# Sinkhorn-sorted attention and a squared-ReLU FFN: the first batch's q transposes, the filler matmuls and the opening order of the head pairs

## The chip, the cores and the metric

One core of a Trainium2 chip runs the whole program. The metric is device microseconds for one execution, and lower is better. TensorE is called PE below, VectorE DVE, ScalarE ACT, GpSimd POOL and SyncE SP, as in the profile.

## What is computed

For each of 4 batches and 8 heads, an 8x8 matrix is put through five rounds of exponential, row normalization and column normalization (Sinkhorn). It then mixes the eight blocks (96 rows each) of k and of v. Each q block attends to its own mixed block, and the result, put back to 3072 tokens of 512 channels, goes through a feed-forward network (FFN).

```python
for _ in range(5):
    P = P - np.max(P, axis=-1, keepdims=True)
    P = np.exp(P)
    P = P / (np.sum(P, axis=-1, keepdims=True) + 1e-09)
    P = P / (np.sum(P, axis=-2, keepdims=True) + 1e-09)
k_sorted = np.einsum('bhij,bhjcd->bhicd', P, k_b).reshape(B, H, S, D)   # v likewise
scores = scale * np.matmul(q_b, k_sb.transpose(0, 1, 2, 4, 3))
attn = softmax(scores); o = np.matmul(attn, v_sb)                       # B,H,S,D = 4,8,768,64
x = o.transpose(0, 2, 1, 3).reshape(3072, 512)
h = np.maximum(x @ w_in, 0.0)                                           # w_in 512 x 2048
out = h * h @ w_out                                                     # w_out 2048 x 512
```

## The kernel before

The work is cut into pieces, and each piece is handed to a planner (`Plan`, lines 50 to 117) as an `Op` with an engine, a cost in microseconds and the ops it depends on. The planner lays all ops out in time with these costs. For PE it has two queues: attention ops, strictly in the order in which they were added, and FFN ops. It takes the attention op at the head when that one is due (its `due` against the number of FFN chunks so far) and nearly ready, or when the FFN could not go on. The instructions are then issued in the order of the planned begins (line 836), so this order is what the engines run; the waits between them are put in by the framework.

A head pair (two heads) of one batch is a `Unit`. Its stages, with the letters that the string `FIRST` (line 19) uses, are:

- q (`s_q`, L385): twelve PE transposes of q into the PSUM tile `qtp` (L395), then a copy to `qT`.
- K and V (`s_sort`, L423): twelve matmuls of k or v with `w_all`, which holds the Sinkhorn weights spread over blocks (L437, tile `tp`), then a cast to `ksT` or `vsT`.
- S (`s_sc`, L461): eight score matmuls into `scp` (L473), then two exponentials on ACT (L489), one for each head, into `et`.
- T (`s_vt`, L497): transposes of the mixed v (L505, tile `vbp`), then a copy to `vs`.
- A (`s_av`, L570): eight matmuls into `oup` (L584), then a reciprocal and a multiply on DVE (L594, L595), the norm, into `ao`.
- X (`s_xt`, L614): transposes of `ao` into `xtp` (L632), then a copy to `xT`, which the FFN reads.

A capital letter in `FIRST` puts the copy on ACT, a small one on DVE.

The FFN runs over 8 groups of 384 tokens (`ffn_unit`, L650). A group has 16 up chunks of four matmuls (L663, tile `hp`), each followed by a ReLU on ACT (L671) and a square on DVE (L674), and then 12 down chunks (L691).

The opening: the sort matrix arrives, five Sinkhorn rounds alternate between ACT (`exp`, L331) and DVE (L299 to L301), then PE transposes and spreads the result (L343, L349) and DVE multiplies it into `w_all` (L360). In the meantime q, k and v of batch 0 arrive by DMAs that POOL issues in a fixed order (lines 258 to 286): q's first 64 partitions (which are the first half of the sequence's blocks), k and v of head pairs 0 to 3, the first quarter of `w_in`, q's second 64 partitions, the rest of `w_in`, `w_out`, then batch 1. ACT also makes `sel` (L308) from the identity that POOL builds between its first two DMAs. PE transposes the first half of q for the four head pairs during Sinkhorn (line 745). Then `FIRST` runs the stages of the first half of batch 0's tokens, and only when its last X is done can the FFN start. The second half of batch 0 is laid between the FFN chunks of group 0 (`lay(0, (1,), ...)`, line 821), and there each unit starts with the transposes of its second half of q (line 793).

While nothing else is there for PE, it runs filler matmuls on a tile of ones: 20 of 256 columns at the start (`warm`, L319), and, until the first FFN chunk, some before each op ahead of which the planner sees a gap of more than 0.5 us:

```python
if filled and not started and op.gap > 0.5:
    fill(int(op.gap / 0.12), 128)
```

PSUM is shared out in three pools: `ps1` with one buffer (`qtp`, `pT`, `vbp`, `xtp`), `ps2` with two buffers of [128, 2, 512] fp32 (`scp`, `oup`, later `tp`, `vnp`), and `psf` with three buffers of [128, 512] fp32 (`pt_ps`, the early `tp`, the FFN's `hp` and `op`, and the fillers' tile `fill`). The planner mirrors them with the rings `r1`, `r2` and `rf` (lines 33 to 47).

Of the kernel before, what the change touches and what calls it, by code (L numbers as in the profile page):

```python
# [8 lines left out]
FP32 = mybir.dt.float32  # L9
BF16 = mybir.dt.bfloat16  # L10
# [5 lines left out]

FIRST = ("V0 K0 v1 K1 t0 S0 k2 v2 S1 t1 A0 V3 K3 t2 S2 S3 t3 A1 X0 A2 X1 A3 X2 x3")


class Op:
# [98 lines left out]
def kernel(  # L121
# [12 lines left out]
    B, H, S, D = q.shape  # L134
# [3 lines left out]
    NA = S // 128  # L138
    C0 = 128 // NB
# [12 lines left out]
    att = ctx.enter_context(tc.tile_pool(name="att", bufs=2))  # L152
    ffn = ctx.enter_context(tc.tile_pool(name="ffn", bufs=2))
    ps1 = ctx.enter_context(tc.tile_pool(name="ps1", bufs=1, space=bass.MemoryType.PSUM))
    ps2 = ctx.enter_context(tc.tile_pool(name="ps2", bufs=2, space=bass.MemoryType.PSUM))
    psf = ctx.enter_context(tc.tile_pool(name="psf", bufs=3, space=bass.MemoryType.PSUM))


    ctx.enter_context(tc.manual_schedule(engines={
        mybir.EngineType.PE, mybir.EngineType.DVE, mybir.EngineType.Activation,  # L160
        mybir.EngineType.SP}))

    plan = Plan()
    rvn, rvb = Ring(2), Ring(3)
# [28 lines left out]
    nc.sync.dma_start(out=p_sb, in_=sort_net.rearrange("b h i j -> (b h) i j"))  # L193


    ones = const.tile([128, 256], BF16)
    nc.vector.memset(ones, 1.0)  # L197
    ident = const.tile([128, 128], BF16)
    nc.vector.memset(ident, 0.0)
# [58 lines left out]
    first = plan.add("DMA", 4.3, lambda e: None)  # L258
    landed["last"] = first
    load(0, 0, 0, H, slice(0, 64))  # L260
    id_op = plan.add("POOL", 0.4, lambda e: make_identity(nc, ident, nomemset=True))
    mask = const.tile([128, C0], BF16)

# [11 lines left out]
        if g == 0:  # L275
            plan.add("POOL", 1.0, make_mask, [id_op])
    load_w_in(0)
    load(0, 0, 0, H, slice(64, 128))
    for g in range(1, 4):
        load_w_in(g)  # L280
    for g in range(4):
# [31 lines left out]
    def fill(n, w):  # L313
        for _ in range(n):
            nc.tensor.matmul(  # L315
                out=tiles["fill"][:, 0:w], lhsT=ones[:, 0:128], rhs=ones[:, 0:w],
                start=True, stop=True)

    def warm(e):  # L319
        tiles["fill"] = psf.tile([128, 512], FP32, tag="pf", name="fill")  # L320
        fill(20, 256)


    slot, old = rf.take()
    rf.use(slot, plan.add("PE", 4.3, warm, [plan.add("DVE", 1.1, lambda e: None)]))

    exps = []
    step = plan.add("SP", 2.25, lambda e: None)
# [1 line left out]
    for it in range(5):  # L330
        step = plan.add("ACT", 0.26, lambda e: nc.scalar.activation(  # L331
            out=p_sb, in_=p_sb, func=AF.Exp), [step])
        exps.append(step)
        if it == 0:
            plan.add("ACT", 0.9, make_sel, [step, id_op])
        step = plan.add("DVE", 0.72, lambda e: sink_norm(e, 0), [step])
        step = plan.add("DVE", 0.76, lambda e, it=it: sink_norm(e, 1, it == 4), [step])

# [44 lines left out]
    def s_q(b, hp, p0, p1, due=0, after=None, eng=AD):  # L385

        n = p1 - p0
        t = {}

        def mm(e):  # L390
            qb = qkv[b][0]
            t["p"] = ps1.tile([128, NA, n], BF16, tag="p1", name="qtp")
            for a in range(NA):
                for h in range(2):
                    nc.tensor.transpose(  # L395
                        out=t["p"][64 * h:64 * (h + 1), a, :],
                        in_=qb[p0:p1, 2 * hp + h, D * a:D * (a + 1)],
                        identity=ident[p0:p1, p0:p1])
            if p0 == 0:
                tiles["qT", b, hp] = att.tile(  # L400
                    [128, NB, NA, C0], BF16, tag="qT", name="qT", bufs=6)

        def ev(e):
            copy(e, tiles["qT", b, hp][:, p0 // C0:p1 // C0, :, :],
                 t["p"].rearrange("p a (i c) -> p i a c", c=C0))

        if b == 0:
            dep = landed[b, 0, 0, p0]
        else:
            dep = landed[b, 0, HP * (2 * hp // HP), 0]  # L410
        s1, old = r1.take()
        if p0 == 0:
            qTs[b, hp], oldq = rqT.take()
        else:
            oldq = []
        pe = plan.add("PE", 0.04 + 0.0023 * n, mm, [dep, id_op] + old, due, mode="col")
        readers[b].append(pe)
        op = one_of(eng, cost_b(NA * n), ev, [pe, after] + oldq)
        r1.use(s1, pe, op)
        rqT.use(qTs[b, hp], op)  # L420
        return op

    def s_sort(u, t, due=0, early=False, eng=AD):  # L423

        st = {}

        def mm(e):
            src = qkv[u.b][t]
            if early:
                tp = psf.tile([128, 512], FP32, tag="pf", name="tp")  # L430
                tp = tp[:, 0:NA * u.ni * C0].rearrange("p (a x) -> p a x", a=NA)
            else:
                tp = ps2.tile([128, NA, u.ni * C0], FP32, tag="p2", name="tp")
            st["p"] = tp
            for a in range(NA):
                for h in range(2):
                    nc.tensor.matmul(  # L437
                        out=tp[64 * h:64 * (h + 1), a, :],
                        lhsT=src[:, 2 * u.hp + h, D * a:D * (a + 1)],
                        rhs=w_all[:, H * u.b + 2 * u.hp + h, u.i0:u.i0 + u.ni, :]  # L440
                        .rearrange("p i c -> p (i c)"),
                        start=True, stop=True)

        def ev(e):
            h0 = u.halves[0]
            copy(e, (u.ksT if t == 1 else u.vsT)[:, h0:h0 + len(u.halves), 0:HS]
                 .rearrange("p h (x a) -> p h x a", a=NA),
                 st["p"].rearrange("p a (h x) -> p h x a", x=NQ * C0))

        h0 = 2 * u.hp  # L450
        dep = landed[u.b, t, h0 if u.b == 0 else HP * (h0 // HP), 0]
        ring = rf if early else r2
        s2, old = ring.take()
        pe = plan.add("PE", 0.336 if u.full else 0.2, mm,
                      [dep, built[H * u.b + h0], built[H * u.b + h0 + 1]] + old, due, mode="col")
        readers[u.b].append(pe)
        op = one_of(eng, cost_f(NA * C0 * u.ni), ev, [pe] + u.old)
        ring.use(s2, pe, op)
        return op

    def s_sc(u, due=0):  # L461
# [3 lines left out]
        for hf in u.halves:  # L465
            st = {}

            def mm(e, hf=hf, st=st):
                qT = tiles["qT", u.b, u.hp]
                st["p"] = scp = ps2.tile([128, 2, 512], FP32, tag="p2", name="scp")  # L470
                for n in range(NQ):
                    for h in range(2):
                        nc.tensor.matmul(  # L473
                            out=scp[:, h, BLK * n:BLK * (n + 1)],
                            lhsT=u.ksT[64 * h:64 * (h + 1), hf, BLK * n:BLK * n + 128],
                            rhs=qT[64 * h:64 * (h + 1), NQ * hf + n, :, :]
                            .rearrange("p a c -> p (a c)"),
                            start=True, stop=True)

            s2, old = r2.take()  # L480
            u.et[hf], olde = ret.take()
            pe = plan.add("PE", 0.17, mm, [u.k_op, u.q_op] + old, due, mode="row")
            r2.use(s2, pe)
# [38 lines left out]
    def s_vn(b, g, due):  # L522
# [3 lines left out]
        for hp in (2 * g, 2 * g + 1):  # L526
            st = {}

            def mm(e, hp=hp, st=st):
                st["p"] = ps2.tile([128, 2, 512], FP32, tag="p2", name="vnp")  # L530
                for h in range(2):
                    nc.tensor.matmul(  # L532
                        out=st["p"][:, h, 0:NA * D],
                        lhsT=w_all[:, H * b + 2 * hp + h, :, :].rearrange("p i c -> p (i c)"),
                        rhs=qkv[b][2][:, 2 * hp + h, :],
                        start=True, stop=True)
# [3 lines left out]
                copy(e, vn_r[m][:, :, h0:h0 + 2, 0:D],  # L540
                     st["p"][:, :, 0:NA * D].rearrange("p e (a d) -> p a e d", d=D))

            s2, old = r2.take()
            h0 = H * b + 2 * hp
            pe = plan.add("PE", 0.34, mm, [landed[b, 2, HP * g, 0], built[h0], built[h0 + 1]]
                          + old, due)
# [23 lines left out]
    def s_av(u, due=0):  # L570
# [4 lines left out]
        for hf in u.halves:  # L575
            st = {}

            def mm(e, hf=hf, st=st):
                if hf == u.halves[0]:
                    u.ao = att.tile([96, u.ni, 2, D], BF16, tag="ao", name="ao", bufs=3)  # L580
                st["p"] = oup = ps2.tile([128, 2, 512], FP32, tag="p2", name="oup")
                for n in range(NQ):
                    for h in range(2):
                        nc.tensor.matmul(  # L584
# [13 lines left out]
                    in1=rec[:, :, :, None].to_broadcast([96, 2, NQ, D]),  # L598
                    op=ALU.mult)

            s2, old = r2.take()
            pe = plan.add("PE", 0.26, mm, u.exps[hf] + [u.vs_op] + old
                          + (olda if hf == u.halves[0] else []), due)
            op = plan.add("DVE", 0.9, norm, [pe])
# [137 lines left out]

    qops = {}
    for hp in range(HP):
        qops[hp] = s_q(0, hp, 0, 64, after=exps[3 + hp // 2], eng="ACT")
    s1, old = r1.take()
    pe = plan.add("PE", 0.12, p_trans, [step] + old)
    op = plan.add("DVE", 0.18, lambda e: nc.vector.tensor_copy(out=p_ij, in_=tiles["pT"]), [pe])
# [36 lines left out]
    def lay(b, halves, c0, c1):  # L785
        step, gap = (c1 - c0) / (HP + 0.9), (c1 - c0 - 13) / (HP - 1)
        for hp in range(HP):
# [2 lines left out]

            def open_(due, b=b, hp=hp, box=box):
                u = box["u"] = Unit(b, hp, halves)
                u.q_op = s_q(b, hp, C0 * u.i0, C0 * (u.i0 + u.ni), due)
                if b == 1:
                    build_w(H * b + 2 * hp, 2, pt, kops[b - 1, hp])
                u.k_op = kops[b, hp] = s_sort(u, 1, due)
                if b < 2:
                    u.v_op = s_sort(u, 2, due)
# [37 lines left out]
    for op in plan.run():  # L836
        if op.eng == "PE":
            started = started or op in plan.ffn
            if filled and not started and op.gap > 0.5:
                fill(int(op.gap / 0.12), 128)  # L840
            filled = True
        op.fn(op.eng)

# [29 lines left out]
```

## Time and profile before

| What | Before |
|---|---|
| median of 6 runs | 236.19 us (235.04 to 239.0) |
| the profiled execution | 235.04 us, its span 233.3 us |
| PE busy | 223.5 us (96%), 2237 matmuls |
| DVE, ACT, POOL busy | 108.4, 124.8, 27.7 us |
| granted TensorE clock | 1.000 |
| FFN matmuls, L663 and L691 | 92.3 and 82.2 us |
| q transposes L395, 240 matmuls | 9.3 us on PE |
| filler matmuls L315, 74 | 8.8 us on PE |
| Sinkhorn's last DVE op begins | 10.84 us |
| last copy to `xT` before the FFN | 21.90 us, for 0.36 us |
| first FFN matmul | 23.12 us |

The span runs from the first to the last instruction; the profiled execution has another 1.74 us around it. A row of the timeline gives the start, the duration, the engine, the line, the operation with the tile it writes and those it reads, and in brackets how long the engine had been idle before it and who ended that. A matmul's row is made of pipelined instructions, so the distance from one start to the next says more than the duration.

### The profile page before, as it was taken

Reading aid. Unit: us, or ns where it says so; the run is one execution under the profiler, and the core shown is the slowest. Engines: PE = TensorE matmul, PEld = TensorE weight load, DVE = VectorE, ACT = ScalarE, POOL = GpSimd, SP = SyncE. Lnnn points to the kernel's source line nnn. Section 1 sums busy time; section 2 is a strip of 40 time slices with the busy share of each in tenths; the row PEclk is TensorE's granted clock in tenths of the full one; section 3 lists DMA queues with packets and bytes.
Section 4 is the critical chain, followed back from the end, with each engine's and each line's share of the span. In section 5 each row is a group of like instructions: output and inputs, shape, how many; then the busy total and the mean of one; then the engine's idle time right before and its main releaser. Section 6 shows DMA issues by size and latency. Waiting matters only on the chain.

```text
span 233.3 us, 5407 instructions
## 1 busy us (share of the span) xinstructions
PE 223.5 (96%) x2237; PEld 130.8 (56%) x2251; DVE 108.4 (46%) x301; ACT 124.8 (53%) x260; POOL 27.7 (12%) x44
## 2 busy tenths in 40 slices
PE   7887999999999999999899999999999999999994
PEld 5766665556666556445565456445665556446553
DVE  6676777327775425205587425205674225105400
ACT  4475675238785247319665347319876257227521
POOL 7953221600006100000000000000000000000000
PEclk9999999999999999999999999999999999999999
DMA  5999999999914993024611240025512330011012
GB/s 78 200 204 206 207 206 204 203 235 230 152 34 71 202 228 78 0 90 185 142 38 37 79 124 0 3 90 200 126 37 46 89 106 0 25 68 45 0 45 91
DMA packets 33143, 25.67 MB, mean 110 GB/s; under 512 B 9952, under 2 KB 29664, under 8 KB 33120
## 3 DMA queue, kind: packets, MB, share of 16 engines
q0 software_dynamic: 16960, 13.63, 37.7%
q1 hardware_dynamic: 16160, 11.71, 17.8%
q8 instruction: 17, 0.28, 0.5%
q14 instruction: 6, 0.05, 0.1%
HBM read 28.89 MB, written 7.91 MB: 158 GB/s over the span
## 4 chain that ended last, share of the span: by engine, by line
PE 85%; DVE 5%; DMA 4%; ACT 3%; issue 1%; ACTq 0%; DVEq 0%
PE op L691 34%; PE hp L663 33%; PE tp L437 4%; PE oup L584 3%; PE scp L473 3%; PE qtp L395 3%; DMA v_way<-vn 2%; DMA vblk<-v_way 2%; PE vbp L505 2%; PE op L725 2%; ACT h L671 1%; DVE p_sb L301 1%; PE vnp L532 1%; PE xtp L632 1%; DMA p_sb<-in_sort_net_dram 1%
## 5 line engine op out<-in xcount | busy, mean ns | idle before, releaser
L663 PE MATMUL hp<-xT,w_in_bf 128*128 128x384 bf16 x512 | 92.3, 326 | 0.0
L691 PE MATMUL op<-w_out_bf,h 128*128 128x512 bf16 x354 | 82.2, 379 | 0.8 <-issue 0.2
L671 ACT ACTIVATE h<-hp 128x384 bf16<-128x384 f32 x128 | 62.7, 494 | 22.9 <-PE hp L663 22.0
L674 DVE TENSOR_TENSOR h<-h 128x384 bf16<-128x384 bf16 x128 | 44.1, 355 | 51.8 <-ACT h L671 51.8
L663 PEld LDWEIGHTS <-w_in_bf 128*128 128x128 bf16 x512 | 46.6, 98 | 29.7
L691 PEld LDWEIGHTS <-h 128*128 128x128 bf16 x368 | 34.7, 98 | 39.0
L180 ACT COPY ob<-op 128x512 f32<-128x512 f32 (+1 forms) x24 | 13.6, 568 | 60.3 <-PE op L691 57.6
L489 ACT ACTIVATE et<-scp 96x384 bf16<-96x384 f32 x64 | 26.5, 490 | 8.7 <-PE scp L473 8.6
L595 DVE TENSOR_TENSOR ao<-oup,rec 96x512 bf16<-96x512 f32 x32 | 22.0, 687 | 1.1
L180 ACT CAST ksT<-tp 128x768 bf16<-128x768 f32 (+1 forms) x17 | 11.4, 671 | 5.3 <-PE tp L437 4.9
L584 PEld LDWEIGHTS <-et 96*128 96x128 bf16 x256 | 10.8, 97 | 4.6 <-DMA vblk<-v_way 1.3
L182 DVE CAST vn<-vnp 128x768 bf16<-128x768 f32 x4 | 3.8, 958 | 19.6 <-PE vnp L532 19.6
L594 DVE RECIPROCAL rec<-oup 96x8 f32<-96x8 f32 x32 | 6.4, 199 | 10.5 <-PE oup L584 10.2
L182 DVE COPY qT<-qtp 128x768 bf16<-128x768 bf16 (+1 forms) x12 | 5.9, 489 | 11.0 <-PE qtp L395 10.9
L473 PEld LDWEIGHTS <-ksT 64*128 64x128 bf16 x256 | 6.3, 94 | 7.8 <-ACT h L671 2.2
L236 POOL DMA_DIRECT2D qb<-in_q_dram x8 | 6.0, 756 | 38.3 <-PE qtp L395 32.4
L473 PE MATMUL scp<-qT,ksT 64*128 64x96 bf16 x256 | 10.1, 205 | 0.5 <-ACT ksT L180 0.2
L395 PEld LDWEIGHTS <-qb 128*64 128x64 bf16 (+1 forms) x240 | 6.9, 109 | 6.6 <-issue 6.0
L395 PE MATMUL qtp<-ident,qb 128*64 128x128 bf16 (+1 forms) x240 | 9.3, 212 | 1.1 <-ACT qT L180 0.6
L315 PE MATMUL fill<-ones 128*128 128x128 bf16 (+1 forms) x74 | 8.8, 283 | 1.2 <-DVE ones L197 1.2
L182 DVE COPY vs<-vbp 96x512 bf16<-96x512 bf16 (+1 forms) x12 | 6.1, 508 | 7.0 <-PE vbp L505 6.9
L437 PE MATMUL tp<-w_all,kb 128*64 128x128 bf16 (+1 forms) x240 | 9.1, 211 | 0.0
(59 smaller groups left out, 125.8 us busy)
## 6 DMA issues: line engine op xcount, KB each, us to landing
out_dram<-ob SPq DMA_DIRECT2D x23, 256.0 KB, 2.0
qb<-in_q_dram POOLq DMA_DIRECT2D x8, 384.0 KB, 13.3
vb<-in_v_dram POOLq DMA_DIRECT2D x6, 384.0 KB, 15.2
kb<-in_k_dram POOLq DMA_DIRECT2D x6, 384.0 KB, 16.3
w_in_bf<-in_moe_w_in_dram POOLq DMA_DIRECT2D x4, 512.0 KB, 12.7
w_out_bf<-in_moe_w_out_dram POOLq DMA_DIRECT2D x4, 512.0 KB, 19.1
v_way<-vn SPq DMA_DIRECT2D x4, 396.0 KB, 3.3
vblk<-v_way SPq DMA_DIRECT2D x4, 396.0 KB, 4.4
```

The lines of the kernel that those rows point to most:

```text
L180: nc.scalar.copy(out=out, in_=in_)
L182: nc.vector.tensor_copy(out=out, in_=in_)
L395: nc.tensor.transpose(out=t["p"][64 * h:64 * (h + 1), a, :], in_=qb[p0:p1, 2 * hp + h, D * a:D * (a + 1)], identity=ident[p0:p1, p0:p1])
L437: nc.tensor.matmul(out=tp[64 * h:64 * (h + 1), a, :], lhsT=src[:, 2 * u.hp + h, D * a:D * (a + 1)], rhs=w_all[:, H * u.b + 2 * u.hp + h, u ...
L473: nc.tensor.matmul(out=scp[:, h, BLK * n:BLK * (n + 1)], lhsT=u.ksT[64 * h:64 * (h + 1), hf, BLK * n:BLK * n + 128], rhs=qT[64 * h:64 * (h ...
L489: nc.scalar.activation(out=et[:, h, 0:HS].rearrange("p (n c a) -> p n c a", c=C0, a=NA), in_=st["p"][0:96, h, 0:HS].rearrange("p (n a c) - ...
L584: nc.tensor.matmul(out=oup[:, h, 66 * n:66 * n + D + 1], lhsT=et_r[u.et[hf]][:, h, BLK * n:BLK * n + 128], rhs=(u.vs[:, NQ * hf + n, h, 0: ...
L595: nc.vector.tensor_tensor(out=u.ao[:, n0:n0 + NQ, :, :].rearrange("p n e d -> p e n d"), in0=ov[:, :, :, 0:D], in1=rec[:, :, :, None].to_b ...
L663: nc.tensor.matmul(out=t["hp", nt][:, 0:HS], lhsT=w_in_bf[:, kc, 128 * nt:128 * (nt + 1)], rhs=xT[:, kc, t0:t0 + HS], start=(kc == 0), sto ...
L671: nc.scalar.activation(out=t["h1", nt], in_=t["hp", nt][:, 0:HS], func=AF.Relu)
L674: nc.vector.tensor_tensor(out=t["h2"][:, nt, :], in0=t["h1", nt], in1=t["h1", nt], op=ALU.mult)
L691: nc.tensor.matmul(out=t["op", mt], lhsT=t["h2"][:, nt, 128 * mt:128 * (mt + 1)], rhs=w_out_bf[:, nt, :], start=(nt == 0), stop=(nt == NT ...
```

## The change

Four things are changed, all before or around the start of the FFN.

1. Both halves of batch 0's q are transposed during Sinkhorn. The DMA of q's second 64 partitions is issued as the second one, ahead of the identity and of k and v. The transposes of batch 0 use `psf` (three buffers) in place of `ps1` (one), all their copies are on ACT, and the units of batch 0's second half no longer begin with transposes.
2. The two `ps2` buffers become two fixed tiles, `p2[0]` and `p2[1]`, taken by the slot number of the ring. The fillers no longer have a `psf` buffer; they write columns 384 to 511 of the second half of `p2[0]`, which no other matmul writes.
3. The fillers: 40 of 128 columns at the start in place of 20 of 256; later ones before each gap of more than 0.15 us, one for each 0.08 us of it.
4. A new `FIRST`, and smaller planned costs for the two Sinkhorn normalizations.

```diff
-FIRST = ("V0 K0 v1 K1 t0 S0 k2 v2 S1 t1 A0 V3 K3 t2 S2 S3 t3 A1 X0 A2 X1 A3 X2 x3")
+FIRST = ("K0 V0 k1 v1 S0 t0 S1 k2 V2 t1 A0 S2 K3 t2 A1 V3 X0 A2 S3 t3 x1 A3 X2 x3")
...
-    ps2 = ctx.enter_context(tc.tile_pool(name="ps2", bufs=2, space=bass.MemoryType.PSUM))
+    ps2 = ctx.enter_context(tc.tile_pool(name="ps2", bufs=1, space=bass.MemoryType.PSUM))
...
+    p2 = [ps2.tile([128, 2, 512], FP32, name=f"p2_{n}") for n in range(2)]
...
-    ones = const.tile([128, 256], BF16)
+    ones = const.tile([128, 128], BF16)
...
     load(0, 0, 0, H, slice(0, 64))
+    load(0, 0, 0, H, slice(64, 128))
     id_op = plan.add("POOL", 0.4, lambda e: make_identity(nc, ident, nomemset=True))
...
     load_w_in(0)
-    load(0, 0, 0, H, slice(64, 128))
...
-                out=tiles["fill"][:, 0:w], lhsT=ones[:, 0:128], rhs=ones[:, 0:w],
+                out=p2[0][:, 1, 512 - w:512], lhsT=ones[:, 0:128], rhs=ones[:, 0:w],
...
-        tiles["fill"] = psf.tile([128, 512], FP32, tag="pf", name="fill")
-        fill(20, 256)
-    slot, old = rf.take()
-    rf.use(slot, plan.add("PE", 4.3, warm, [plan.add("DVE", 1.1, lambda e: None)]))
+        fill(40, 128)
+    plan.add("PE", 4.3, warm, [plan.add("DVE", 1.1, lambda e: None)])
...
-        step = plan.add("DVE", 0.72, lambda e: sink_norm(e, 0), [step])
-        step = plan.add("DVE", 0.76, lambda e, it=it: sink_norm(e, 1, it == 4), [step])
+        step = plan.add("DVE", 0.66, lambda e: sink_norm(e, 0), [step])
+        step = plan.add("DVE", 0.69, lambda e, it=it: sink_norm(e, 1, it == 4), [step])
...
-            t["p"] = ps1.tile([128, NA, n], BF16, tag="p1", name="qtp")
+            if b == 0:
+                t["p"] = psf.tile([128, NA, n], BF16, tag="pf", name="qtp")
+            else:
+                t["p"] = ps1.tile([128, NA, n], BF16, tag="p1", name="qtp")
...
-                tp = ps2.tile([128, NA, u.ni * C0], FP32, tag="p2", name="tp")
+                tp = (p2[s2].rearrange("p b x -> p (b x)")[:, 0:NA * u.ni * C0]
+                      .rearrange("p (a x) -> p a x", a=NA))
...
-        qops[hp] = s_q(0, hp, 0, 64, after=exps[3 + hp // 2], eng="ACT")
+        qops[hp] = s_q(0, hp, 0, 64, after=exps[2 + (hp + 2) // 3], eng="ACT")
+    q2ops = [s_q(0, hp, 64, 128, after=exps[4], eng="ACT") for hp in range(HP)]
...
-                u.q_op = s_q(b, hp, C0 * u.i0, C0 * (u.i0 + u.ni), due)
+                u.q_op = q2ops[hp] if b == 0 else s_q(b, hp, 0, 128, due)
...
-            if filled and not started and op.gap > 0.5:
-                fill(int(op.gap / 0.12), 128)
+            if filled and not started and op.gap > 0.15:
+                fill(int(op.gap / 0.08), 128)
```

The tiles `scp`, `vnp` and `oup` take `p2[slot]` in the same way as `tp`. For the other batches the transposes, their tile and their place are as before.

More of the change, by code (lines that the diff above doesn't have):

```diff
@@ L410, in s_q @@
             dep = landed[b, 0, HP * (2 * hp // HP), 0]
-        s1, old = r1.take()
+        ring = rf if b == 0 else r1
+        s1, old = ring.take()
         if p0 == 0:
@@ L418, in s_q @@
         op = one_of(eng, cost_b(NA * n), ev, [pe, after] + oldq)
-        r1.use(s1, pe, op)
+        ring.use(s1, pe, op)
         rqT.use(qTs[b, hp], op)
@@ L466, in s_sc, with mm @@
             st = {}
-            def mm(e, hf=hf, st=st):
+            slot, old = r2.take()
+            def mm(e, hf=hf, st=st, slot=slot):
                 qT = tiles["qT", u.b, u.hp]
-                st["p"] = scp = ps2.tile([128, 2, 512], FP32, tag="p2", name="scp")
+                st["p"] = scp = p2[slot]
                 for n in range(NQ):
@@ L478, in mm @@
                             start=True, stop=True)
-            s2, old = r2.take()
+            s2 = slot
             u.et[hf], olde = ret.take()
@@ L527, in s_vn, with mm @@
             st = {}
-            def mm(e, hp=hp, st=st):
-                st["p"] = ps2.tile([128, 2, 512], FP32, tag="p2", name="vnp")
+            slot, old = r2.take()
+            def mm(e, hp=hp, st=st, slot=slot):
+                st["p"] = p2[slot]
                 for h in range(2):
@@ L541, in ev @@
                      st["p"][:, :, 0:NA * D].rearrange("p e (a d) -> p a e d", d=D))
-            s2, old = r2.take()
+            s2 = slot
             h0 = H * b + 2 * hp
@@ L576, in s_av, with mm @@
             st = {}
-            def mm(e, hf=hf, st=st):
+            slot, old = r2.take()
+            def mm(e, hf=hf, st=st, slot=slot):
                 if hf == u.halves[0]:
                     u.ao = att.tile([96, u.ni, 2, D], BF16, tag="ao", name="ao", bufs=3)
-                st["p"] = oup = ps2.tile([128, 2, 512], FP32, tag="p2", name="oup")
+                st["p"] = oup = p2[slot]
                 for n in range(NQ):
@@ L599, in norm @@
                     op=ALU.mult)
-            s2, old = r2.take()
+            s2 = slot
             pe = plan.add("PE", 0.26, mm, u.exps[hf] + [u.vs_op] + old
```

## The prediction, made before the change was run

> **What bounds the kernel.** I read the busy time of the engines by stretches first.
>
> ```profile
> core 0: us, PE busy (x) PEld busy (x) DVE busy (x) ACT busy (x) POOL busy (x), PEclk, DMA share, GB/s
> 6.00:12.00 6.00, 4.99 (x102) 4.25 (x101) 3.97 (x19) 2.36 (x7) 6.00 (x10) 1.00 1.31 200
> 16.00:22.30 6.30, 4.68 (x100) 3.64 (x97) 4.94 (x13) 4.33 (x11) 1.66 (x3) 1.00 1.27 206
> 22.30:30.00 7.70, 7.68 (x132) 4.98 (x131) 5.85 (x16) 4.71 (x11) 2.25 (x4) 1.00 1.24 207
> 30.00:40.00 10.00, 9.95 (x151) 6.37 (x148) 7.26 (x21) 6.88 (x16) 1.48 (x3) 1.00 1.27 205
> ```
>
> From 22.3 us on PE is full, so PE work taken out there shortens the run one for one, and so does an earlier start of the FFN. Before that PE idles or runs fillers, and the chain of waits goes through Sinkhorn and the first head pairs. The granted clock is 1.00 in every row. So the whole effect is (a) PE work taken out behind 22.3 us and (b) the shift of the first FFN matmul. For both, PE's timeline around the FFN's start:
>
> ```profile
> 21.54 0.33 PE L632 MATMUL xtp<-ident,ao 96*128 96x96 bf16 x4 [0.29 <-ACT xT L180]
> 22.32 0.38 PE L395 MATMUL qtp<-ident,qb 64*64 64x64 bf16 x12 [0.45 <-DVE xT L182]
> 22.62 0.38 PE L437 MATMUL tp<-w_all,kb 128*64 128x64 bf16 x12
> 22.83 0.36 PE L437 MATMUL tp<-w_all,vb 128*64 128x64 bf16 x12
> 23.12 0.82 PE L663 MATMUL hp<-xT,w_in_bf 128*128 128x384 bf16 x4
> ...
> 27.34 0.38 PE L395 MATMUL qtp<-ident,qb 64*64 64x64 bf16 x12
> 27.65 0.38 PE L437 MATMUL tp<-w_all,kb 128*64 128x64 bf16 x12
> ```
>
> The q transposes sit between X and the FFN, and wait 0.45 us because they need the one `ps1` buffer that the last X still holds. Last, the timeline of all engines in the opening:
>
> ```profile
> 2.16 0.31 POOL masks.py:199 TENSOR_SCALAR_AFFINE_SELECT ident<-ident 128x128 bf16<-128x128 bf16 x1
> ...
> 2.51 1.04 ACT L308 COPY sel<-ident 64x1024 bf16<-64x1024 bf16 x1
> ...
> 4.04 0.26 ACT L331 ACTIVATE p_sb<-p_sb 32x64 f32<-32x64 f32 x1 [0.49 <-DVE p_sb L301]
> ...
> 12.03 0.42 DVE L360 TENSOR_TENSOR w_all<-mask,pt_ps 128x256 bf16<-128x256 bf16 x1 [0.52 <-PE pt_ps L349]
> ...
> 12.48 0.37 ACT L753 CAST pt<-pt_ps 128x256 bf16<-128x256 f32 x1 [1.48 <-DVE w_all L360]
> ...
> 13.46 0.38 PE L437 MATMUL tp<-w_all,vb 128*64 128x64 bf16 x12 [0.17 <-ACT vsT L180]
> ```
>
> Two things to see: `sel` starts right after the identity and ends 0.49 us before the second exponential; and the third sort matmul waits for the cast of the first, so of three `psf` buffers only two turn (the third is the fillers').
>
> **q's second half, taken out of the full stretch.** Four groups of twelve transposes go. The three later ones cost their distance to the next op: 27.34 to 27.65, 33.21 to 33.51, 39.29 to 39.60, together 0.92 us. PE has at most 0.07 us of idle time in the two rows behind 22.3 us, so nothing refills this. The first one costs 0.30 and the 0.45 wait, but what then comes late is the last copy to `xT` (21.90 + 0.36 = 22.26): K and V run at 21.75 and 21.95 and the FFN starts at 22.32 rather than 23.12. **0.80 us**. The copies (0.36 to 0.48 us) were not limiting there.
>
> **The same work put into Sinkhorn.** PE has 1 us idle from 6 to 12 us and over 2 us of fillers; ACT is busy 2.36 of 6. Eight copies at 0.41 us from start to start: one after the third exponential, three between the fourth and the fifth (7.82 to 9.33 us, 1.51 us of room for 1.3), four behind the fifth, done some 1 us before the `pt` copy. At nothing; the cover is thin only in the middle group, and each 0.1 us over would cost 0.1.
>
> **The DMA order.** q's second half is issued before the identity, one POOL issue of 0.74 us (its row at 9.62). The identity then ends at about 3.2, `sel` runs 3.22 to 4.26, and the second exponential, behind it on ACT, starts at 4.28 instead of 4.04. Sinkhorn is one chain: **0.24 us later** from there on. k and v land later by q's transfer, about 1.9 us (k1 lands 1.9 us after k0, and one k and one v part are as many bytes): k0 9.0, v2 13.9, k3 14.8, v3 17.1 (before 7.1, 12.0, 12.9, 15.2); `w_in`'s first quarter 19.8. From its second quarter (22.1) on nothing moves. SP's queue is not passed.
>
> **The new order.** I laid the new `FIRST` out with the trace's distances: operand to PE 0.06 us, PE to its copy 0.42 (S 0.39, T 0.44, A 0.46, X 0.37), a cast or copy on ACT 0.41 from start to start, on DVE 0.47 (T 0.34), the norm 0.83, an exponential 0.41, a sort matmul group 0.21. With Sinkhorn at +0.24, `w_all` stands at 12.69 and `pt` at 13.09 (the copy waits for DVE as before). K0 12.74, V0 12.95, k1 13.62, S0 14.15, S1 14.75, A0 15.83, S2 16.32, A1 17.28, V3 17.55, A2 17.96, t3 19.1. DVE is full from 14.1 to 20.0 and sets A0, A1, A2. S3 needs `p2[0]` back from A1's norm (18.65). Its exponentials end at 20.0, A3 20.13, norm to 21.5, x3 21.69, copy to 22.41. From `w_all` that is 9.72 us, in the old trace 22.26 - 12.45 = 9.81. So the third buffer and the order give **0.09 us** only: DVE and ACT take up what PE no longer waits for. Error of this by hand: 0.5 us either way.
>
> **The fillers.** At the start 40 of 128 columns are as many columns as 20 of 256; some 52 before q's first half lands end at about 6.9 us instead of 6.4 (28 with 6144 columns took 5.25 us), off the chain. The others now write into `p2[0]`. [...] The nearest row is `pt`'s copy above: ACT and DVE only read `pt_ps`, and ACT waits for DVE's end (12.45) to start at 12.48. It agrees that the program orders such pairs, but no row shows a filler and a reader.
> Where it bites: by the planner's costs PE has, in the chain's end, a gap of 0.19 us before S3 (2 fillers) and one of 0.60 us before x1 (t3 ends at 18.66 on its clock, x1 waits for t3's copy until 19.26: 7 fillers). Both come after readers of `p2[0]`: A1's norm and S3's exponentials. The gap is spent waiting, and the fillers run after it, 55 ns each (in the old trace 7 take 0.56 us and 5 take 0.45). S3 0.11 later, its exponentials end 20.11; then 7 fillers, x1 at 20.56, and A3 behind it at 20.76 rather than 20.13: x3's copy ends at 23.05. Queued behind x1: A3, X2, x3 and the FFN. [...]
>
> **The sum.** FFN's start: -0.80 + 0.24 - 0.09 + 0.64 = -0.01 (23.11); work taken out -0.92. Together -0.93: 235.04 becomes 234.1 for the profiled execution (span 232.4, 1.74 around it). That execution was the fastest of six; on the median, 236.19 - 0.93 = **235.3 us**.
>
> **Rivals.**
> *The corner is free.* Fillers do not wait. The FFN starts at 22.47: -0.65 - 0.92 = -1.57, **234.6 us**. For it: the columns are disjoint. [...]
> *The late v3 decides (slower).* V3 is in PE's order ahead of X0, A2, S3, t3. By my layout it may land as late as 17.7 before x3 moves; I put it at 17.1. In the old trace it needed 7.0 us from issue where its neighbours needed 5.0 to 5.5, since it lands among `w_in`'s packets. If it drags to the landing of `w_in`'s first quarter (19.8), PE stands 2.1 us there: -0.93 + 2.1 = +1.2, **237.4 us**. It turns the sign from a landing at 18.6 on.
> *The moved work doesn't count.* PE's freed 0.92 us comes back as waits for ACT or PSUM in the FFN, and the start stays: **236.2 us**. Against it: 0.02 and 0.05 us idle in the stretches with the old load, and less load for ACT and DVE there now.
>
> **How the numbers follow.** Fillers wait 0.45, corner free 0.38, late v3 0.12, no effect 0.05. A measurement of this kernel can tell about 0.5% from no change, that is 1.18 us, so faster means below 235.0. The first case, with 0.5 us of error by hand, puts 0.13 below it, 0.29 within and 0.03 above; the second 0.31 below and 0.07 within; the third is slower, the fourth the same. Faster 0.44, same 0.41, slower 0.15. The range reaches from 233.8 (the free corner and its error) to 236.7 (the first case's error, the fourth case and the mild part of the third); it leaves out the rest of the late v3 and some of the tails, about 0.18.
>
> **What the changed profile would show.** No `qtp` between 22 and 50 us, and K straight behind the last X. `sel` at about 3.2 and the second exponential at 4.28; Sinkhorn's last DVE op at 11.08. [...] V3's row waiting for a DMA, if v3 is late. First FFN matmul at 23.1 (22.5 without the waits), and from there to the end 0.92 us less than before. I am wrong if the planner's new times also reorder PE behind 50 us: the one long wait there, 1.0 us for `vblk`, could grow or go, though due numbers, not times, fix the order around it.

## The result

The changed kernel takes 235.18 us in the median of 29 runs (234.56 to 237.41). Beside it the kernel before took 236.91 us (62 runs, 235.01 to 239.33). The ratio is 0.9949, with a 95% interval from 0.9931 to 0.9967: 1.2 us less. That ratio is one of means, and it leaves out the eight slow executions of the kernel before, those more than 1.5% above its fastest, so it is nearer to 1 than the two medians. The forecast had been 235.3 us. As the rest shows, that agreement was luck: errors of opposite sign cancel.

The profiled execution took 236.21 us, its span 233.8. First the stretches of the changed kernel, to be held against those shown of before; the column to look at is the granted clock (PEclk).

```profile
core 0: us, PE busy (x) PEld busy (x) DVE busy (x) ACT busy (x) POOL busy (x), PEclk, DMA share, GB/s
6.00:12.00 6.00, 5.63 (x144) 4.55 (x145) 3.97 (x19) 3.84 (x11) 5.54 (x9) 1.00 1.31 202
16.00:22.30 6.30, 4.42 (x90) 3.66 (x89) 4.04 (x10) 3.81 (x10) 2.47 (x4) 0.91 1.24 207
22.30:30.00 7.70, 7.64 (x113) 5.69 (x113) 4.99 (x13) 3.97 (x10) 2.22 (x3) 0.85 1.24 207
30.00:40.00 10.00, 10.00 (x128) 6.35 (x128) 7.38 (x22) 7.50 (x18) 2.96 (x4) 1.00 1.27 205
```

From 6 to 12 us PE is busier than before (5.63 against 4.99 us). From 16 us on it is not, and its clock falls. PE's timeline shows what lies ahead of that. A row's bracket gives its idle time and what ended it; "issue" means that nothing in the profile did.

```profile
17.94 0.35 PE L443 MATMUL tp<-w_all,vb 128*64 128x64 bf16 x10
...
19.48 0.22 PE L443 MATMUL tp<-w_all,vb 128*64 128x64 bf16 x2 [1.20 <-issue]
...
20.28 0.34 PE L481 MATMUL p<-qT,ksT 64*128 64x96 bf16 x8
...
20.71 0.38 PE L513 MATMUL vbp<-ident,vsT 128*128 128x128 bf16 x4
...
21.59 0.91 PE L318 MATMUL p<-ones 128*128 128x128 bf16 x7 [0.49 <-ACT et L497]
...
22.28 0.53 PE L644 MATMUL xtp<-ident,ao 96*128 96x96 bf16 x4
```

Two things cost time. V3 stops for 1.20 us between its tenth and eleventh matmul, though all twelve read the same load of v. And seven fillers ahead of x1 wait for S3's second exponential (`et`) and then run in front of x1, as the prediction had it. Their row lasts 0.91 us, at a granted clock of 0.50 (21.59 to 22.30 us).

The start of the FFN, in the PE timeline of the changed kernel:

```profile
24.43 0.41 PE L644 MATMUL xtp<-ident,ao 96*128 96x96 bf16 x4
24.77 0.38 PE L443 MATMUL p<-w_all,kb 128*64 128x64 bf16 x12
24.98 0.36 PE L443 MATMUL p<-w_all,vb 128*64 128x64 bf16 x12
25.27 0.82 PE L675 MATMUL hp<-xT,w_in_bf 128*128 128x384 bf16 x4
```

K stands straight behind the last X, and no `qtp` follows until 52 us. From X to the FFN it is 0.84 us instead of 1.58. But the FFN starts 2.15 us later than in the old trace. From there to the end it takes 208.53 us instead of 210.18.

One more term moved, which the traces do not show: the time outside the span. In the executions of the kernel before it is 1.70 to 1.83 us (59 of them), in those of the changed kernel 1.92 to 2.56, 2.35 on the mean (40 of them): 0.6 us more.

The clock differs from execution to execution, for both kernels, and that decides the comparison. All executions of the two kernels whose clock was recorded, over all the comparisons made here, with their time and span:

| mean granted clock | before: executions, mean us (span) | changed: executions, mean us (span) |
|---|---|---|
| 0.997 to 1.000 | 7, 234.83 (233.09) | 22, 235.00 (232.66) |
| 0.990 to 0.993 | 16, 236.00 (234.21) | 12, 236.02 (233.60) |
| 0.983 to 0.986 | 25, 237.39 (235.62) | 6, 237.19 (234.93) |
| 0.978 and less | 11, 238.31 (236.54) | none |

At equal clock the two kernels take the same time within 0.2 us: the changed one's span is 0.4 to 0.7 us shorter, and the time outside it takes that back. What differs is how often the clock stays up: 7 of 59 against 22 of 40. These counts come from different comparisons; in the one that has both kernels side by side with their clocks they are 1 of 25 against 3 of 10. With the old kernel's time for each class and the changed kernel's shares, the mean would be 235.57 us, against 236.88 for the old and 235.63 measured for the changed one: on these figures the shares make all of the gain.

### The profile page after: what moved, and what is told of

It is laid out like the page before. It is cut to its first block, busy times and chain, and to the rows that moved or that the text cites. A ratio compares the mean times of both kernels' runs of the same rounds, so it can differ in the third digit from the quotient of the medians.

```text
span 233.8 us, 5519 instructions
## 1 busy us (share of the span) xinstructions
PE 225.1 (96%) x2283; PEld 133.5 (57%) x2296; DVE 107.8 (46%) x298; ACT 125.5 (54%) x263; POOL 27.7 (12%) x44
## 3 DMA queue, kind: packets, MB, share of 16 engines
q0 software_dynamic: 16960, 13.63, 37.7%
## 4 chain that ended last, share of the span: by engine, by line
PE 88%; DVE 4%; DMA 2%; ACT 2%; issue 2%; ACTq 0%; DVEq 0%; POOLq 0%
PE hp L675 34%; PE op L703 34%; PE qtp L399 3%; PE p L481 3%; PE p L443 3%; PE p L596 3%; PE p L318 2%; DMA qb<-in_q_dram 2%; PE op L737 1%; PE vbp L513 1%; DVE ao L607 1%; ACT h L683 1%; DVE h L686 1%; PE p L542 1%; DVE vn L185 1%
## 5 line engine op out<-in xcount | busy, mean ns | idle before, releaser
L497 ACT ACTIVATE et<-p 96x384 bf16<-96x384 f32 x64 | 26.6, 489 | 9.3 <-PE p L481 9.3
L607 DVE TENSOR_TENSOR ao<-p,rec 96x512 bf16<-96x512 f32 x32 | 22.0, 687 | 1.3 <-DVE rec L606 0.2
L318 PE MATMUL p<-ones 128*128 128x128 bf16 x119 | 11.4, 255 | 1.5 <-DVE ones L200 1.1
L185 DVE CAST vn<-p 128x768 bf16<-128x768 f32 x4 | 3.8, 958 | 19.6 <-PE p L542 19.6
L606 DVE RECIPROCAL rec<-p 96x8 f32<-96x8 f32 x32 | 6.4, 200 | 11.0 <-PE p L596 9.2
L183 ACT CAST ksT<-p 128x768 bf16<-128x768 f32 (+1 forms) x13 | 9.5, 730 | 3.6 <-PE p L443 3.5
L481 PE MATMUL p<-qT,ksT 64*128 64x96 bf16 x256 | 10.2, 205 | 0.3 <-DVE ao L607 0.2
L318 PEld LDWEIGHTS <-ones 128*128 128x128 bf16 x119 | 9.0, 117 | 2.0 <-DVE ones L200 1.1
L399 PEld LDWEIGHTS <-qb 128*64 128x64 bf16 (+1 forms) x240 | 6.4, 109 | 5.5 <-issue 4.0
L185 DVE COPY qT<-qtp 128x768 bf16<-128x768 bf16 x8 | 4.5, 556 | 10.1 <-PE qtp L399 10.1
```

The costliest lines, as they stand in the source:

```text
L183: nc.scalar.copy(out=out, in_=in_)
L185: nc.vector.tensor_copy(out=out, in_=in_)
L318: nc.tensor.matmul(out=p2[0][:, 1, 512 - w:512], lhsT=ones[:, 0:128], rhs=ones[:, 0:w], start=True, stop=True)
L399: nc.tensor.transpose(out=t["p"][64 * h:64 * (h + 1), a, :], in_=qb[p0:p1, 2 * hp + h, D * a:D * (a + 1)], identity=ident[p0:p1, p0:p1])
L481: nc.tensor.matmul(out=scp[:, h, BLK * n:BLK * (n + 1)], lhsT=u.ksT[64 * h:64 * (h + 1), hf, BLK * n:BLK * n + 128], rhs=qT[64 * h:64 * (h ...
L497: nc.scalar.activation(out=et[:, h, 0:HS].rearrange("p (n c a) -> p n c a", c=C0, a=NA), in_=st["p"][0:96, h, 0:HS].rearrange("p (n a c) - ...
```

## The experiments

My theory after the traces: the q part saves what was forecast; the fillers on the readers' bank and the stop in V3 give it back; the denser fillers keep the clock up. The rivals: the stop is late data of v3 or chance; the gain is the q part.

**The changed kernel again.** No edit.

> The changed kernel once more, for a second trace. In its first trace V3 stops after ten of its twelve matmuls for 1.2 us, with nothing of the data missing, and then TensorE's clock falls to 0.85 to 0.91. Theory (PE waits for its next block of instructions, since more of them are used up in the opening): the stop comes again at the same matmul, 1.0 to 1.6 us, FFN start at 24.3 to 25.3 us. Rival (a chance event of that execution): no stop, FFN start at 23.2 to 23.6, and the time 235.1 of most executions belongs to that.

Median 235.85 us (10 runs), ratio 0.9948 (0.9913 to 0.9983). PE's timeline:

```profile
17.87 0.35 PE L443 MATMUL tp<-w_all,vb 128*64 128x64 bf16 x10
18.96 0.22 PE L443 MATMUL tp<-w_all,vb 128*64 128x64 bf16 x2 [0.74 <-issue]
...
24.87 0.82 PE L675 MATMUL hp<-xT,w_in_bf 128*128 128x384 bf16 x4
```

The stop comes at the same matmul, so it is no chance, only shorter (0.74) than I expected. The FFN starts within the expected range. The three executions at full clock took 234.66 us on the mean. Neither of the two traces of this kernel is at full clock (0.991 and 0.992).

**No late fillers.** `first_k` is K0's matmuls.

```diff
-            if filled and not started and op.gap > 0.15:
+            opened = opened or op is first_k
+            if filled and not opened and op.gap > 0.15:
```

> No fillers behind the first sort matmuls. Theory (fillers wait for the readers of p2[0] and run after the gap): S3 0.1 and A3 0.5 to 0.6 earlier against their exponentials, so 0.6 us less than the changed kernel at full clock; the stop in V3 stays. Rival (the late fillers keep the clock up): the clock falls in more executions and the time is the same or up to 1 us more.

Median 236.56 us, ratio 0.9964 (0.9931 to 0.9997). No execution kept the full clock (0.983 to 0.993). At 0.993 it took 235.55 us, against 235.95 for the changed kernel at 0.990 to 0.992 in the same comparison, so the late fillers cost some 0.4 us at nearly equal clock, where 0.6 was expected. From S3 to A3 it is 1.65 us instead of 2.13 (the repeat) and 2.33. But the late fillers also hold the clock, and the rival was right about the sum. That the stop stays in V3 was wrong:

```profile
17.52 0.38 PE L443 MATMUL tp<-w_all,vb 128*64 128x64 bf16 x12
17.83 0.34 PE L646 MATMUL xtp<-ident,ao 96*128 96x96 bf16 x4
18.01 0.23 PE L598 MATMUL p<-vs,et 96*128 96x65 bf16 x2
19.18 0.36 PE L598 MATMUL p<-vs,et 96*128 96x65 bf16 x6 [0.95 <-issue]
```

The stop has left V3 and stands after A2's second matmul. Eight fillers fewer run ahead of it (two before v1, six before K0), that is 16 instructions, a weight load and a matmul each. From V3's tenth matmul to A2's second it is two, four and two matmuls: 16 instructions again. The stop belongs to a place in PE's instruction stream, behind 351 matmuls with a weight load each, and not to an operation or its data. That speaks against late data of v3.

**Wide early fillers.** Ahead of K0 half as many fillers, of 256 columns:

```diff
-        fill(40, 128)
+        fill(20, 256)
...
+                if opened:
+                    fill(int(op.gap / 0.08), 128)
+                else:
+                    fill(int(op.gap / 0.08 + 1) // 2, 256)
```

> Fillers ahead of the first sort matmuls are half as many and twice as wide (256 columns), the same columns; PE has 90 instructions less before V3. Theory (instruction blocks): the stop leaves V3, where the next block is now needed some 3 us later, and is gone or under 0.3 us: FFN start 1.2 to 1.5 us earlier than in the changed kernel's trace, time 1.2 us less. Rival (v3's data or DMA load stops V3): V3 stops as before, time the same.

Median 234.28 us (4 runs, all at clock 1.000), ratio 0.9881 (0.9831 to 0.9931). No row of PE waits for "issue". V3 runs its twelve matmuls at 18.50 in one piece, and the FFN starts at 23.92, 1.35 us before that of the changed kernel's trace (which had lost the clock), although Sinkhorn's transpose came 0.55 us later (11.91 after 11.36). That is in part the rounding up; the first q transposes already start 0.48 us later in this trace (6.85 after 6.37).

**The q part alone.** The kernel before, with the load, `psf` and `q2ops` edits of the change, old order and old fillers.

> The kernel before with only the q part: both halves of batch 0's q loaded and transposed in Sinkhorn, old order, old fillers in psf. Theory: 0.92 us less work behind the FFN's start and 0.8 at it, but V3 stands early in the old order and its data lands at about 17.3 where it was needed at 16.1, so 1.0 to 1.3 us of it are given back: 0.4 us faster than before, within 0.8 either way. Rival (the order is no matter): 1.5 us faster. Third (two psf buffers only for q, since the fillers hold one, delays Sinkhorn): slower by 0.5 or more.

Median 236.97 us, ratio 1.0010 (0.9976 to 1.0043). The time lies in the wide range of the first expectation, but not for its reason: PE does not wait for v3's data. None of the three had the clock. The stretches of this kernel:

```profile
6.00:12.00 6.00, 4.66 (x119) 3.77 (x117) 3.81 (x18) 3.72 (x10) 5.78 (x9) 0.82 1.31 201
12.00:16.00 4.00, 3.35 (x64) 2.71 (x59) 1.62 (x4) 1.71 (x4) 2.23 (x4) 0.50 1.31 203
16.00:22.30 6.30, 6.04 (x129) 4.84 (x124) 3.73 (x9) 3.83 (x10) 2.22 (x3) 0.68 1.24 207
```

The clock stood at half from before 12 to after 16 us, and every execution was at 0.971 or 0.978. At 0.978 it took 236.86 us (7 executions), where the old kernel at 0.977 to 0.978 takes 238.15 (9 executions). So at equal clock the q part saves 1.3 us, if lost clock costs the same wherever it falls, and it needs the fillers to show it.

**Wide, and not too many.** As the wide run, with `fill(int(op.gap / 0.19), 256)` ahead of K0.

> Wide early fillers as in the wide-filler run, but one of 256 columns for each 0.19 us of a gap, rounded down, so that Sinkhorn's transpose doesn't wait for them; late fillers as in the change. Theory (wide fillers take the stop in V3 away and hold the clock; they made the Sinkhorn transpose 0.55 us late): transpose at 11.3 in place of 11.9, FFN start at 23.3 to 23.5, 233.8 us at full clock, 0.4 to 0.6 under the wide-filler run. Rival (their density held the clock): clock 0.985 to 0.993 in half of the executions and 1.1 us more in each of those.

Median 234.15 us (5 runs, all at 1.000), ratio 0.9882 (0.9815 to 0.9949); transpose at 11.24, FFN start at 23.24. The clock speaks for the theory; the time is 0.3 above its forecast and only 0.1 under the wide run, where 0.4 to 0.6 was expected. The trace of the wide run is the slowest of its four executions (234.89 us, the others 234.00 to 234.47), so its late transpose may not stand in the others.

**Fillers that wait for nobody.** In addition, each late filler takes the bank whose last reader ends first by the plan, and only the time left after it:

```diff
-                    fill(int(op.gap / 0.08), 128)
+                    at = min(read, key=lambda x: read[x])
+                    room = op.begin - max(op.begin - op.gap, read[at])
+                    fill(int(max(room, 0) / 0.08), 128, at)
...
+        for at in getattr(op, "reads", ()):
+            read[at] = op.end
```

> As the run before, and each late filler goes to the bank of the two tiles whose last reader ends first by the plan, and only for the time that is left after that reader. Theory (fillers that wait for readers cost 0.6 us): FFN start 0.5 to 0.7 us before that of the run beside it, 233.2 us. Rival (the exponentials, not the fillers, set x1 and A3): FFN start within 0.2 us of it. Third (fewer fillers let the clock fall): 1.1 us more for each 3.4 us at half clock.

Median **233.47 us** (5 runs, clock 0.998 to 1.000), ratio 0.9850 (0.9792 to 0.9909). It beats both kernels. PE's timeline, first of the run before and then of this one:

```profile
20.41 0.55 PE L318 MATMUL p<-ones 128*128 128x128 bf16 x7 [0.63 <-ACT et L499]
20.80 0.34 PE L646 MATMUL xtp<-ident,ao 96*128 96x96 bf16 x4
...
23.24 0.82 PE L677 MATMUL hp<-xT,w_in_bf 128*128 128x384 bf16 x4
```

```profile
19.81 0.44 PE L318 MATMUL p<-ones 128*128 128x128 bf16 x5 [0.22 <-DVE ao L610]
20.14 0.33 PE L648 MATMUL xtp<-ident,ao 96*128 96x96 bf16 x4
...
22.57 0.82 PE L679 MATMUL hp<-xT,w_in_bf 128*128 128x384 bf16 x4
```

x1 comes 0.66 us earlier and the FFN 0.67. So that is the price of the late fillers, against 0.64 in the prediction; the edit moves them and also drops two before S3 and two before x1, and the two parts are not told apart. The five that are left still wait 0.22 us for a norm. This FFN start is 0.10 from the 22.47 of the prediction's rival with a free corner, in which no filler waits.

**Dense fillers alone.** The kernel before with two numbers changed:

```diff
-            if filled and not started and op.gap > 0.5:
-                fill(int(op.gap / 0.12), 128)
+            if filled and not started and op.gap > 0.15:
+                fill(int(op.gap / 0.08), 128)
```

> The kernel before with only the thresholds of the fillers changed (from 0.15 us on, one for 0.08 us), in their old psf buffer; old order, q as before. Theory (the change's gain is the clock that stays up in more executions): mean clock 0.992 to 1.000 instead of 0.978 to 0.993, 1 to 2 us less in the median, 234.9 at full clock as before. Rival (the gain is the q work taken out of the full stretch): clock and time as before, within 0.5 us.

Median 235.23 us (11 runs, clock 0.998 to 1.000 in all of them; beside it the old kernel had that in 1 of 15), ratio 0.9933 (0.9902 to 0.9965). The theory holds: without any of the q part, the order or the corner, this has the whole gain of the change. The time outside the span is 1.78 us here, as before.

```profile
16.00:22.30 6.30, 6.06 (x133) 4.88 (x130) 5.28 (x13) 5.06 (x13) 1.83 (x4) 1.00 1.27 206
```

PE is busy for 6.06 of these 6.30 us, where the kernel before has 4.68. The fillers aren't free: ten ahead of Sinkhorn's transpose make it start at 11.70 instead of 11.11, and the FFN at 23.84 instead of 23.12.

**The old order in the changed kernel.** Only `FIRST` is put back.

> The changed kernel with the old order of the head pairs. Theory (the new order is there because k and v land 1.9 us later): V3, fifth from the front in the old order's second half, waits for its data until 17 us and holds what is behind it: FFN start 0.5 to 1.2 us later than in the changed kernel without its stop. Rival (the order does nothing): FFN start within 0.3 us.

Median 239.83 us, ratio 1.0120 (1.0055 to 1.0185); FFN start at 27.41. Both expectations missed, and the cause was not the one I had named:

```profile
PE p L318 <- DVE ao L607: 2.2, 2, 1.1
PE p L318 <- ACT et L497: 1.1, 2, 0.6
```

PE waits 3.3 us in fillers for readers of `p2[0]`, and no row waits for v3. This trace also bounds the theory of the clock:

```profile
16.00:22.30 6.30, 4.57 (x102) 3.55 (x102) 2.74 (x7) 2.99 (x8) 2.36 (x4) 1.00 1.24 208
```

PE is busy for no more of this stretch than in the kernel before, one wait in it lasts 1.09 us, and the clock is 1.00 (in 3 of 5 executions for the whole program). So neither the busy share of one stretch nor one gap of this length decides the clock; what does was not found out here.

**Early fillers narrow again.** The fastest run with `fill(2 * int(op.gap / 0.19), 128)` and `fill(40, 128)`.

> The fastest run so far (wide early fillers, late fillers that wait for nobody), with its early fillers narrow again: twice as many of 128 columns, the same columns and times, 82 PE instructions more. Theory (a block of instructions that comes late): PE stops at the same place in its instruction stream as in the changed kernel, which is here after the fourth of A2's eight matmuls, for 0.5 to 1.3 us; FFN start 0.5 to 1.2 us later, 233.9 to 234.6 us. Rival (the stop came from v3's data or from the timing of the change): no stop, 233.3 to 233.6 us.

Median 234.00 us, ratio 0.9906 (0.9864 to 0.9947).

```profile
18.32 0.29 PE L599 MATMUL p<-vs,et 96*128 96x65 bf16 x4
18.92 0.30 PE L599 MATMUL p<-vs,et 96*128 96x65 bf16 x4 [0.31 <-issue]
...
23.08 0.82 PE L679 MATMUL hp<-xT,w_in_bf 128*128 128x384 bf16 x4
```

The stop is back at the predicted matmul and the FFN starts 0.51 us later. It is shorter than I expected (0.31 us).

**The old order with fillers that wait for nobody.**

> The fastest run so far with the old order of the head pairs. The old order in the changed kernel lost 4 us, with fillers waiting 3.3 us for norms and exponentials. Theory (fillers on the readers' bank were the loss, not the order): FFN start at 22.6 to 23.3, at most 0.7 us later than with the new order. Rival (v3's late landing, 17.1 us, holds the old order up): a wait for v3 of 0.5 us or more ahead of V3 and FFN start 1 us or more later.

Median 236.29 us, ratio 1.0000 (0.9966 to 1.0035), FFN start at 25.26: 2.7 us later. The theory that the order is no matter falls.

```profile
17.14 0.89 PE L318 MATMUL p<-ones 128*128 128x128 bf16 x13 [0.37 <-ACT et L499]
17.96 0.38 PE L443 MATMUL tp<-w_all,vb 128*64 128x64 bf16 x12
```

The old order asks for V3 early; the planner sees a gap of over 1 us there, presumably for v3's data, and puts thirteen fillers into it, and three groups of fillers in all still wait for exponentials (1.3 us). How much of the 2.7 us is data and how much fillers this run doesn't tell.

**The identity first.** The fastest run, with the identity ahead of the load of q's second half.

> The fastest run so far, with the identity made ahead of the load of q's second half. My prediction gave this load's place 0.24 us of delay in Sinkhorn, by way of sel on ACT. By that: the second exponential 0.2 us earlier, FFN start and time 0.2 us less. By the changed kernel's trace (the exponential started 0.05 us after DVE, before sel's row ended): no change, within 0.1 us at the exponential; k and v, issued no earlier, no change either.

Median 233.57 us, ratio 0.9883 (0.9803 to 0.9964), FFN start at 22.66: no change. First to second exponential it is 1.75 us, against 1.77 in the fastest run. Their `sel` ran at 2.50 and 3.19.

## Why the prediction was right in its number and wrong in its account

*q out of the full stretch, 0.92 us.* The groups are gone, but they gave 0.67 us. First two rows of the kernel before, then four of the changed one:

```profile
50.91 0.53 PE L395 MATMUL qtp<-ident,qb 128*64 128x128 bf16 x12
...
115.09 0.67 PE L584 MATMUL oup<-vblk,et 96*128 96x65 bf16 x16 [0.96 <-DMA vblk<-v_way]
```

```profile
29.18 0.69 DVE L607 TENSOR_TENSOR ao<-p,rec 96x512 bf16<-96x512 f32 x1
...
29.49 0.38 PE L443 MATMUL p<-w_all,kb 128*64 128x64 bf16 x12
...
29.92 0.38 PE L443 MATMUL p<-w_all,vb 128*64 128x64 bf16 x12
...
52.39 0.53 PE L399 MATMUL qtp<-ident,qb 128*64 128x128 bf16 x12
```

From the FFN's start to batch 1's first transposes it is 27.12 us (52.39 - 25.27) instead of 27.79 (50.91 - 23.12). In the first of the three groups V comes 0.43 us behind K, where it was 0.21 (27.65 to 27.86): V takes over the slot of `p2` that the norm before it reads, and starts 0.05 us after that norm's end (29.18 + 0.69). So "nothing refills this" was wrong by a quarter, in the way of the third rival. The rest of the 1.65 us is the wait for `vblk` (0.96 us in the old trace), which isn't there; the prediction named it as one that could go. It comes and goes between kernels (0.8 us in the run with dense fillers alone, 0.6 with the old order); I didn't follow up why.

*The FFN's start, 0.80 us.* Right: 1.58 to 0.84 us from the last X to the first FFN matmul, 0.74 less.

*Sinkhorn 0.24 us later by `sel`.* The size came (`w_all` starts at 12.30 instead of 12.03), the mechanism didn't. The rows of ACT in the changed kernel:

```profile
3.19 1.04 ACT L311 COPY sel<-ident 64x1024 bf16<-64x1024 bf16 x1 [0.58 <-POOL ident masks.py:199]
...
4.13 0.25 ACT L332 ACTIVATE p_sb<-p_sb 32x64 f32<-32x64 f32 x1
```

`sel` did move to 3.19, but the next ACT instruction starts at 4.13, before `sel`'s row ends at 4.23, and 0.05 us after DVE's last operand (3.87 + 0.21). I had added rows end to end. The run with the identity first agrees: `sel` moved back and nothing was gained. What came late was Sinkhorn's transpose: `pf` is written at 11.17, 0.12 us later than before (of which 0.07 stand at the first exponential already), and nine fillers held PE until the transpose at 11.36. With fewer fillers it started at 11.24.

*The new order, 0.09 us.* My layout by hand is within 0.4 us until V3: K0 12.74 (measured 12.86), k1 13.62 (13.63), S0 14.15 (14.47), S2 16.32 (16.53), A1 17.28 (17.60), V3 17.55 (17.94). The drift begins between k1 and S0, where two fillers run ahead of v1 (from 13.94). The 0.09 us itself was not measured alone; with the old order the FFN started 2.7 us later, but with other fillers.

*Fillers behind readers, 0.64 us.* Right in kind. No run shows the 0.64 us itself; it was my estimate, on the assumption that a filler waits for every reader of `p2[0]`. What the runs showed in its place: in the changed kernel seven fillers wait 0.49 us for `et`, and their row of 0.91 us stands in front of x1; in the run whose fillers hardly wait x1 comes 0.66 us earlier and the FFN 0.67, though that run took four fillers away as well.

*What was missing.* The stop in PE's instruction stream, 0.74 and 1.20 us. The rival with the late v3 named the place, but not the cause. It comes behind the same 351 matmuls in four traces (0.31 to 1.20 us), leaves V3 when fewer instructions run ahead of it, and returns when they are put back. That a block of instructions comes late there is my inference; no row shows it. Packets of an instruction queue (q8) do run among the data: in the changed kernel one between 17.00 and 17.25 us, with the DMA share at 1.24 from 16.00 to 22.30 us, and the stop ends over 2 us later, at 19.48; in the kernel before one between 18.75 and 19.00 us, and no stop follows. No row says which engine a packet is for.

*The step that failed: the clock.* From the granted clock of 1.00 in every row I took the whole effect to be work and the FFN's start, and gave the fillers no gain. That was one execution, the fastest of six; the 1.7% between the six were the hint. Most executions of the old kernel lose some clock (52 of 59); where in the program, no trace of it shows, but the traces of the changed kernel and of the q part alone lose it in the opening. Denser fillers alone keep it (0.998 to 1.000 in all 11 executions).

At full clock the change brought +0.2 us in place of -0.93. The terms, as far as the record has them:

| term at full clock | predicted | measured |
|---|---|---|
| the FFN's start | -0.01 us | +1.2 us (estimate) |
| from there to the end | -0.92 us | -1.65 us |
| outside the span | 0 (its 1.74 us carried over) | +0.6 us |

The first one is estimated: the mean spans at full clock, less the 208.53 and 210.18 us that the traces have behind the start, put it at 24.13 and 22.91 us. I take some 0.8 of the 1.2 for the stop, since the run with fewer, wide fillers ahead of K0 has no stop and starts the FFN at 23.24; no trace of the changed kernel at full clock shows it. The cause of the 0.6 stays open: all the runs with both halves of q in the opening have some of it (1.97 to 2.53 us outside the span on the mean), the one with dense fillers alone has not.

Over the executions of all clocks the change brought -1.2 us, all from the clock. Without the stop, and with fillers that hardly wait, the same idea gives 233.5, that is 1.4 us less than the old kernel at full clock (234.83), near the -1.57 of the rival with a free corner.

## What to carry to other kernels

Sort the executions by their granted clock before explaining a difference; here the two kernels took equal time within each class (within 0.2 us), and the gain was in the shares. Check the time outside the span too, which no trace shows (here 0.6 us more). Filler matmuls had a price in three places here: they stood in front of real work (with ten ahead of it Sinkhorn's transpose started at 11.70 instead of 11.11 us), they waited for readers of the tile they write, though those read other columns (0.49 us for `et` in the changed kernel), and they used up instructions (the stop behind 351 matmuls, 0.31 to 1.20 us, came and went with their number); the fastest run, with few wide ones that hardly wait, kept the clock (0.998 to 1.000) at 233.47 us. When PE stops with its operands there, count its instructions: a stop that stays behind the same number of instructions while the operation there changes, here from V3 to A2, is hardly a data wait.

## What the runs showed of the hardware that I had not expected

The mean clock comes in steps: 1.000, 0.992, 0.985, 0.978, 0.971. One step of 0.0075 over 233 us is 1.7 us of clock, that is 3.5 us at half clock. In the changed kernel's trace, one step down, the clock is 0.50 from 21.2 to 24.6 us, 3.4 us in one piece, and 1.00 ahead of it and behind it; the two rows with 0.91 and 0.85 lack as much (0.6 and 1.2 us). In the trace of the q part alone, at 0.978, the three rows with 0.82, 0.50 and 0.68 lack 5.1 us together, three steps. From class to class a step costs 0.9 to 1.4 us in this program. What starts such a stretch and what ends it, no run here shows.
